# A planned adaLN transformer block on one core: set-up as planned items, new item weights, x+gb*b2 on TensorE, two gelu phases

## The chip, the cores and the metric

One core of a Trainium2 chip runs the whole program. A core has five engines with a queue each: TensorE (PE, matmuls; PEld is its weight load), VectorE (DVE), ScalarE (ACT), GpSimd (POOL) and SyncE (SP, which here only issues DMAs). The metric is the device time of one execution in microseconds, lower is better; for a kernel it is the median of its runs.

## The reference

2048 tokens of width 448, 16 heads of 28, a hidden width of 1792, all bf16. Each token attends to 8 tokens at distances 0, 2, ..., 14 behind it.

```python
mod = (_silu(c) @ w_mod).reshape(c.shape[0], 6, 1, -1)
sa, ca, ga, sb, cb, gb = (mod[:, 0], mod[:, 1], mod[:, 2], mod[:, 3], mod[:, 4], mod[:, 5])
h = _layernorm(x) * (1 + ca) + sa
x = x + ga * _A_ref(h, A_wqkv, A_wo)      # sliding, dilated attention, then @ wo
h = _layernorm(x) * (1 + cb) + sb
x = x + gb * _B_ref(h, B_w1, B_b1, B_w2, B_b2)
# _B_ref: y = layernorm(h); gelu_tanh(y @ w1 + b1) @ w2 + b2
```

## The kernel before

Even tokens come first and odd ones after them, so that the dilated window is a plain window of 8. The 2048 tokens are 16 blocks (b) of 128 on the partitions; attention works on 17 groups (g) of 121 queries with 128 keys; the MLP on 4 chunks (c) of 512 tokens.

Set-up is written out by hand. SP issues the loads of c, x (blocks 0 to 3), wmod (the part for sa and ca), the staging copy of the q and k weights (wqk_st) and Wv. PE turns c into a column (ps_c), DVE and ACT make silu of it, PE multiplies it with wmod (ps_col, line 326), DVE writes ca1_col and sa_col (lines 334 to 337), and DVE and ACT spread wqk_st into Wqk, with 32 columns for each head of 28. Thirteen idle matmuls on zeros (line 270) are placed around this. The other loads (x_all 4 to 15, wmod2, wo, b2, w1, b1, w2) are issued on SP too, and wait for the load of Wv.

Everything after that is a list of items for a planner (class Plan). An item has a name, the engines it could run on with a duration for each, the items it needs, the items it must not start before, and the buffers that it takes or uses. `order` places the items one by one: of those that are ready it takes the one with the earliest start, and among equals the one with the longest tail of durations behind it; where an item may run on two engines it takes the one that ends first. The items are then emitted in the order of their planned starts. On the chip each engine works through its queue in that order, and waits for semaphores. Load times are given to the planner as estimates (LANDS).

The items, by name and line:

- front end of a block pair or four blocks: `fst` statistics of x (385, with the aggregation on 386), `frs` variance plus eps (`tv`, DVE, 392) and its power -0.5 (`rs`, POOL, 395), `z` normalised into zbuf (400), `zt` transposes on PE into `ptr` (430), `h` scale and shift into hT (ACT 438 or DVE 441), `qk` projections into `pq` (452), `qe` copies into qT and kT (376 or 378).
- attention of a group: `lt` logits in 16 small matmuls (522) into two PSUM tiles of tag lt, `ex` two exponentials (ACT 533) into `et`, `mk` product with mask_rest (DVE 542), `pv` values (557) and `ve` their copy into vbuf, `po` the 16 products (567), `on` reciprocal of the denominator and division (DVE 575 and 577), `pt` transposes (584), `ot` copies into oT.
- block: `wo` output projection (605), `x1` residual (DVE 610).
- norms of a pair of blocks: `s2`, `r2`, `z2` (z on 400), `ml` and `ad` (DVE 629: times 1+cb, plus sb), `s3`, `r3`, `y` (ybuf), `yt` a transposing DMA on SP into yT (644).
- MLP of a chunk: `w1` in 7 items of 8 matmuls (660) into PSUM tiles of the tag lt, `ge` gelu (ACT 667) into hm, `w2` in 7 items of 2 matmuls for each block (686), accumulated into p2, `xp` the sum x + gb*b2 (POOL 677) into x1p_ring, `fin` the last sum (DVE 693), `out` the store.
- modulation: `pb_ga`, `pb_sb`, `pb_cb`, `pb_gb` (475); wo is scaled with ga (483, 485), w2 with gb (499).

PSUM has two tiles of tag lt (two banks each), three of tag s and one of tag p2. The last chunk's second to fourth block use tag s for p2. In SBUF `et` has two buffers. The gelus of a chunk are kept in phases: PHASES gives, for each chunk, the number of attention groups whose exponentials come before its gelus.

```python
PHASES = [10, 13, 16, 17]
SLOTS = {"lt": 2, "s": 3, "p2": 1, "et": 2, "on": 2, "vb": 3, "z2": 2, "yT": 2, "hm": 2, "xp": 4}
wait_for(bulk_dmas, wv_loads[1:], "bulk loads after the critical loads")
```

Of the kernel before, what the change touches and what calls it, by code (L numbers as in the profile page):

```python
# [15 lines left out]
KT = 4  # L16
KA = 64
# [14 lines left out]
PHASES = [10, 13, 16, 17]  # L32
# [3 lines left out]
LANDS = [("x0", 5.0), ("mod1", 9.8), ("wq", 10.5), ("wv", 11.0), ("x4", 14.5), ("wmod2", 19.0), ("wo", 20.0),  # L36
         ("b2", 21.0), ("x8", 24.0), ("w1", 29.0), ("w2", 34.0)]
PLANS = None
SCHED = mybir.DependencyInfo(mybir.DependencyClass.NoSync, mybir.DependencyReason.SCHED_ONLY)
# [4 lines left out]
class Plan:  # L44
# [8 lines left out]
    def add(self, name, eng, needs=(), after=(), uses=(), allocs=(), lag=0.09, tab=None, at=0.0, fn=None, pri=0.0):  # L53

        i = len(self.ops)
        self.index[name] = i
        self.ops.append(dict(name=name, eng=eng, needs=list(needs), after=list(after), allocs=list(allocs), lag=lag,
                             tab=tab, at=at, fn=fn, pri=pri))
        for b in list(uses) + list(allocs):
            self.bufs[b][1].append(i)  # L60

    def order(self, hop=0.07, table=1.3):
# [33 lines left out]
        seq = []  # L96
# [10 lines left out]
        while ready:  # L107
# [31 lines left out]
            start[i], end[i], o["ran"] = s, s + o["eng"][e] + o["lag"], e  # L139
            free[e] = s + o["eng"][e]  # L140
# [18 lines left out]
def kernel(  # L159
# [56 lines left out]
    x1p_ring = cst.tile([128, NX1P, D], FP32, name="x1p_ring")  # L216
# [27 lines left out]
    silu_bf = cst.tile([128, KT], BF16, name="silu_bf")  # L244
    wk = ctx.enter_context(tc.tile_pool(name="wk", bufs=2))
# [7 lines left out]
    nc.sync.dma_start(out=x_all[:, 0:2, :], in_=xv[:, 0, 0:2, :])  # L253
    nc.sync.dma_start(out=x_all[:, 2:4, :], in_=xv[:, 0, 2:4, :])
# [4 lines left out]
    load_ktiles(nc.sync, wqk_st, A_wqkv[:, 0:2 * D], 0)  # L259
    wv_loads = load_ktiles(nc.sync, Wv, A_wqkv[:, 2 * D:3 * D], 0)  # L260
# [40 lines left out]
    ps_c = ps_small([128, KT], FP32, "ps_c")  # L301
    for kt in range(KT):
        nk = 128 if kt < KT - 1 else 64
        nc.tensor.matmul(ps_c[0:nk, kt:kt + 1], lhsT=c_row[0:1, kt * 128:kt * 128 + nk], rhs=one1[0:1, 0:1],
                         start=True, stop=True)
    c_col = stp.tile([128, KT], FP32, name="c_col")
    nc.vector.memset(c_col[:], 0.0)
    nc.vector.tensor_copy(out=c_col[:, 0:KT - 1], in_=ps_c[:, 0:KT - 1])
    nc.vector.tensor_copy(out=c_col[0:64, KT - 1:KT], in_=ps_c[0:64, KT - 1:KT])
    e_c = stp.tile([128, KT], FP32, name="e_c")  # L310
    nc.scalar.activation(out=e_c[:], in_=c_col[:], func=ACT.Exp, scale=-1.0)
    nc.vector.tensor_scalar_add(out=e_c[:], in0=e_c[:], scalar1=1.0)
    nc.vector.reciprocal(out=e_c[:], in_=e_c[:])
    nc.vector.tensor_tensor(out=silu_bf[:], in0=e_c[:], in1=c_col[:], op=ALU.mult)

    idle(6)

# [3 lines left out]
    ps_col = ps_small([128, 2 * KT], FP32, "ps_col")  # L321
    for v in range(2):
        for j in range(KT):
            nj = 128 if j < KT - 1 else 64
            for kt in range(KT):
                nc.tensor.matmul(ps_col[0:nj, v * KT + j:v * KT + j + 1],
                                 lhsT=wmod[0:kr_of(kt), kt, v * D + j * 128:v * D + j * 128 + nj],
                                 rhs=silu_bf[0:kr_of(kt), kt:kt + 1], start=(kt == 0), stop=(kt == KT - 1))
    idle(3)
    ca1_col = cst.tile([128, KT], FP32, name="ca1_col")  # L330
    sa_col = cst.tile([128, KT], FP32, name="sa_col")
    nc.vector.memset(ca1_col[64:128, KT - 1:KT], 0.0)
    nc.vector.memset(sa_col[64:128, KT - 1:KT], 0.0)
    nc.vector.tensor_scalar_add(out=ca1_col[:, 0:KT - 1], in0=ps_col[:, KT:2 * KT - 1], scalar1=1.0)
    nc.vector.tensor_scalar_add(out=ca1_col[0:64, KT - 1:KT], in0=ps_col[0:64, 2 * KT - 1:2 * KT], scalar1=1.0)
    nc.vector.tensor_copy(out=sa_col[:, 0:KT - 1], in_=ps_col[:, 0:KT - 1])
    nc.vector.tensor_copy(out=sa_col[0:64, KT - 1:KT], in_=ps_col[0:64, KT - 1:KT])

    for kt in range(KT):
        kr = kr_of(kt)  # L340
        wq_out = Wqk[0:kr, kt, :, :].rearrange("p m (r e) -> p m r e", e=32)[:, :, :, 0:DH]
        wq_in = wqk_st[0:kr, kt, :].rearrange("p (m r d) -> p m r d", m=8, r=4)
        if kt in (0, 2):
            nc.vector.tensor_copy(out=wq_out, in_=wq_in)
        else:
            nc.scalar.copy(out=wq_out, in_=wq_in)
    nc.vector.tensor_copy(out=silu_bc[:], in_=silu_bf[:].unsqueeze(2).to_broadcast([128, KT, 128]))
    bulk_dmas.append(nc.sync.dma_start(out=x_all[:, 4:8, :], in_=xv[:, 0, 4:8, :]))
    bulk_dmas += load_ktiles(nc.sync, wmod2, w_mod[:, 2 * D:6 * D], 0)
    bulk_dmas += load_ktiles(nc.sync, wo_s, A_wo, ZR_N)  # L350
    bulk_dmas.append(nc.sync.dma_start(out=b2_bc[:], in_=B_b2.partition_broadcast(128)))
    bulk_dmas.append(nc.sync.dma_start(out=x_all[:, 8:NBLK, :], in_=xv[:, 1, :, :]))
# [6 lines left out]
    bulk_dmas += load_ktiles(nc.sync, w1_s, B_w1, 0)  # L359
    bulk_dmas.append(nc.sync.dma_start(out=w1_s[KA:KA + 1, KT - 1, :], in_=B_b1.rearrange("(o n) -> o n", o=1)))  # L360
    bulk_dmas.append(nc.sync.dma_start(out=w2_s[:], in_=B_w2.rearrange("(ft p) n -> p ft n", p=128)))
    wait_for(bulk_dmas, wv_loads[1:], "bulk loads after the critical loads")
    stp_cm.__exit__(None, None, None)
    big = ctx.enter_context(tc.tile_pool(name="big", bufs=2))
# [4 lines left out]
    ALL = list(range(KT))  # L369

    def engine(e):
        return nc.vector if e == "DVE" else nc.scalar
# [7 lines left out]
    def stats(nm, tile_key, n, i, src, **kw):  # L380
        def fn(e):
            if i == 0:
                T["mv", tile_key] = sm.tile([128, n, 2], FP32, name="mv", tag=f"mv{n}")
            st = sm.tile([128, 6], FP32, name="st", tag="st")
            nc.vector.bn_stats(out=st[:], in_=src())  # L385
            nc.vector.bn_aggr(out=T["mv", tile_key][:, i, :], in_=st[:])  # L386
        P.add(nm, {"DVE": 0.62}, fn=fn, **kw)
# [21 lines left out]

    zc = [0]  # L410

    def front_end(b0, nb, x_at):
# [4 lines left out]
        rstd(f"frs{b0}", f, nb, needs=[f"fst{b0 + i}" for i in range(nb)])  # L417
# [17 lines left out]
        for kt in range(KT):  # L435
# [8 lines left out]
            P.add(f"h{b0}.{kt}", {"ACT": 0.45 + 0.0004 * w, "DVE": 0.2 + 0.0005 * w},  # L444
                  needs=[f"zt{b0 + i}" for i in range(nb)] + ["mod1"], uses=[f"ptr{b0}"], fn=h_fn)
        h_of[b0] = [f"h{b0}.{kt}" for kt in range(KT)]
        for m in range(8):
# [6 lines left out]
            P.add(f"qk{b0}.{m}", {"PE": 4 * w / 2400}, needs=h_of[b0] + ["wq"], allocs=[f"pq{b0}.{m}"], lag=0.17,  # L454
# [3 lines left out]
            P.add(f"qe{b0}.{m}", {"ACT": 0.06 + w / 1164, "DVE": 0.07 + w / 960}, needs=[f"qk{b0}.{m}"],  # L458
# [6 lines left out]
    front_end(2, 2, "x0")  # L465
# [4 lines left out]
    def mod_item(idx, nm, use, lens):  # L470
# [7 lines left out]
        P.add(nm, {"PE": 0.76}, needs=["wmod2"], allocs=[nm], lag=0.17, fn=fn)  # L478
# [9 lines left out]
    def use_gb(e, pb):  # L488
        nc.vector.tensor_copy(out=gb_bc[:], in_=pb[:])
        nc.vector.tensor_tensor(out=gbb2_bc[:], in0=pb[:], in1=b2_bc[:], op=ALU.mult)  # L490

    mod_item(2, "pb_ga", use_ga, {"DVE": 2.0})
# [3 lines left out]
    mod_item(5, "pb_gb", use_gb, {"DVE": 1.08})  # L496
# [10 lines left out]
    def attention(g, exp_after, lt_after):  # L507
# [5 lines left out]
        for nm, tag in ((f"lt{g}.0", "lt"), (f"lt{g}.1", "lt"), (f"pv{g}", "s"), (f"po{g}", "s"), (f"pt{g}", "s"),  # L513
                        (f"et{g}", "et"), (f"on{g}", "on"), (f"vb{g}", "vb")):
            P.buf(nm, tag)
# [10 lines left out]
        P.add(f"lt{g}", {"PE": 0.45}, after=lt_after, needs=[f"qe{f}.{m}" for f in fes for m in range(8)], lag=0.17,  # L526
# [34 lines left out]
        P.add(f"ve{g}", {"ACT": 0.47, "DVE": 0.54}, needs=[f"pv{g}"], uses=[f"pv{g}", f"vb{g}"],  # L561
# [7 lines left out]
        P.add(f"po{g}", {"PE": 0.45}, needs=[f"mk{g}", f"ve{g}"], uses=[f"et{g}", f"vb{g}"], allocs=[f"po{g}", f"on{g}"],  # L569
              lag=0.17, fn=o_fn)  # L570

        def d_fn(e):
            rden = sm.tile([128, H], FP32, name="rden", tag="rden")
            po = T["po", g]
            nc.vector.reciprocal(out=rden[:], in_=po[:, :, DH])
            on = T["on", g] = wk.tile([128, D], BF16, name="on", tag="on")
            nc.vector.tensor_tensor(out=on[:].rearrange("p (h d) -> p h d", h=H), in0=po[:, :, 0:DH],  # L577
                                    in1=rden[:].unsqueeze(2).to_broadcast([128, H, DH]), op=ALU.mult)
        P.add(f"on{g}", {"DVE": 0.71}, needs=[f"po{g}"], uses=[f"po{g}", f"on{g}"], fn=d_fn)
# [6 lines left out]
        P.add(f"pt{g}", {"PE": 0.24}, needs=[f"on{g}"], uses=[f"on{g}"], allocs=[f"pt{g}"], lag=0.2, fn=p_fn)  # L586
# [132 lines left out]
    for i in todo:  # L719
        o = P.ops[i]  # L720
        if o["fn"]:
            o["fn"](o["ran"])
# [32 lines left out]
```

## Time and profile before

| | |
|---|---|
| median of 3 runs | 216.62 us (216.28 to 218.09) |
| the profiled execution | 217.38 us, span 215.7 us |
| PE busy | 186.4 us (86%) in 1466 matmuls |
| DVE busy | 142.9 us (66%) |
| ACT busy | 111.8 us (52%), 12 table loads among it |
| POOL busy | 45.2 us (21%) |
| p from yT (w1) | 213 records, 52.0 us |
| p from hm (w2) | 224 matmuls, 46.3 us |
| x1p on POOL | 16, 18.9 us |
| statistics (385) and aggregation (386) | 48 each, 29.4 and 8.7 us |
| HBM read and written | 9.18 and 1.84 MB |

The span is the time from the first to the last instruction of the profiled execution; its own time holds a little more around it. A row of the timeline gives the start and the length in us, the engine, the line, the operation, the tiles (written <- read), the number of instructions merged, and in brackets the idle time of the engine before it and what ended that. Matmuls overlap, so that the length of one is more than the step from it to the next; some matmul records are missing (11 of the 224 w1 matmuls).

### The profile page before, as it was taken

The page shows a single profiled execution, that of the slowest core. Times are in us where ns is not written, and L with a number is a line of the kernel's source. Part 1 is how long each engine was busy: PE and PEld are TensorE (multiplying, and loading weights), DVE is VectorE, ACT ScalarE, POOL GpSimd, SP SyncE. Part 2 cuts the span into 40 slices and gives each one's busy share as a digit, 9 for nine tenths or more (in the row PEclk, how much of TensorE's full clock was granted, in tenths as well). Part 3 has the DMA queues.
Part 4 walks back from the last instruction along what each step waited for, and adds up shares of the span by engine and source line. Part 5 has one row for each costly group of instructions (what it writes and reads, how often), then busy time and mean ns, then how long its engine had stood idle before and what let it go on. Part 6 is the DMA issues. An engine that isn't in the chain of part 4 may idle for free.

```text
span 215.7 us, 3681 instructions
## 1 busy us (share of the span) xinstructions
PE 186.4 (86%) x1466; PEld 96.4 (45%) x1481; DVE 142.9 (66%) x327; ACT 111.8 (52%) x142; POOL 45.2 (21%) x72
## 2 busy tenths in 40 slices
PE   7247994999999789988596999998999888999973
PEld 2225862355446335534243454544544443445531
DVE  2076697979999887899998868626788671000232
ACT  3033876373897856859327759467793301531000
POOL 8502010010311020107434401303041151000130
PEclk9755997699999999999979999999999999999999
DMA  4959994000002011000113110110000212000011
GB/s 118 292 152 365 345 292 146 0 0 3 0 2 52 0 27 24 2 3 0 24 25 74 39 34 0 32 38 24 21 24 2 49 48 65 3 0 0 28 61 62
DMA packets 17973, 13.35 MB, mean 62 GB/s; under 512 B 9250, under 2 KB 17059, under 8 KB 17956
## 3 DMA queue, kind: packets, MB, share of 16 engines
q1 hardware_dynamic: 17956, 13.12, 21.2%
q8 instruction: 11, 0.18, 0.3%
q14 instruction: 6, 0.05, 0.1%
HBM read 9.18 MB, written 1.84 MB: 51 GB/s over the span
## 4 chain that ended last, share of the span: by engine, by line
PE 55%; DVE 31%; POOL 4%; DMA 3%; ACT 2%; issue 2%; SPq 1%; POOLq 0%
PE p L686 16%; PE pq L452 13%; PE p L660 12%; DVE st L385 6%; POOL rs L395 4%; PE pv L557 4%; PE pw L605 4%; DVE z L629 3%; DMA wmod<-in_w_mod_dram 3%; DVE x_all L693 3%; DVE z L400 2%; DVE et L542 2%; DVE on L577 2%; DVE mv L386 2%; DVE x_all L610 2%
## 5 line engine op out<-in xcount | busy, mean ns | idle before, releaser
L660 PE MATMUL p<-yT,w_s 128*128 128x512 bf16 x213 | 52.0, 385 | 1.6 <-ACT et L533 0.9
L686 PE MATMUL p<-w_s,hm 128*128 128x448 bf16 x224 | 46.3, 353 | 6.2 <-DVE x_all L693 6.2
L667 ACT ACTIVATE hm<-p 128x1024 bf16<-128x1024 f32 x28 | 28.6, 1023 | 35.9 <-PE p L660 35.7
L395 POOL TENSOR_TENSOR rs<-tv,neg_half 128x2 f32<-128x2 f32 (+1 forms) x21 | 19.3, 923 | 111.3 <-DVE tv L392 111.3
L533 ACT ACTIVATE et<-lt 128x1024 bf16<-128x1024 f32 x34 | 33.4, 1027 | 6.8 <-PE lt L522 6.7
L452 PE MATMUL pq<-hT,Wqk 128*128 128x512 bf16 (+1 forms) x156 | 33.0, 360 | 3.1 <-DVE wo_s L485 1.7
L686 PEld LDWEIGHTS <-hm 128*128 128x128 bf16 x224 | 21.2, 98 | 27.2 <-issue 7.9
L660 PEld LDWEIGHTS <-w_s 128*128 128x128 bf16 x224 | 21.8, 99 | 25.9 <-issue 2.4
L693 DVE TENSOR_TENSOR x_all<-p,x1p_ring 128x448 bf16<-128x448 f32 x16 | 10.0, 623 | 35.0 <-PE p L686 31.4
L677 POOL TENSOR_TENSOR x1p_ring<-x_all,gbb_bc 128x448 f32<-128x448 bf16 x16 | 18.9, 1186 | 52.7 <-DVE x_all L693 49.4
L452 PEld LDWEIGHTS <-Wqk 128*128 128x128 bf16 x160 | 15.9, 104 | 16.9 <-issue 5.0
L542 DVE TENSOR_TENSOR et<-et,mask_rest 128x2048 bf16<-128x2048 bf16 x17 | 21.4, 1258 | 1.0 <-ACT et L533 1.0
L385 DVE BATCH_NORM_STATS2 st<-x_all 128x6 f32<-128x448 bf16 x32 | 19.6, 612 | 0.2
L557 PE MATMUL pv<-Wv,hT 128*128 128x448 bf16 x68 | 15.3, 353 | 0.1
L605 PE MATMUL pw<-wo_s,oT 128*128 128x448 bf16 x64 | 15.2, 362 | 0.2
L610 DVE TENSOR_TENSOR x_all<-pw,x_all 128x448 bf16<-128x448 f32 x16 | 9.9, 617 | 4.5 <-PE pw L605 4.3
L378 ACT CAST kT<-pq 128x512 bf16<-128x512 f32 (+1 forms) x18 | 9.3, 517 | 4.4 <-PE pq L452 4.0
L577 DVE TENSOR_TENSOR on<-po,rden 128x448 bf16<-128x448 f32 x17 | 10.6, 625 | 0.6
L378 ACT CAST vbuf<-pv 128x448 bf16<-128x448 f32 x14 | 7.4, 536 | 6.8 <-PE pv L557 6.7
L438 ACT ACTIVATE hT<-ptr,sa_col,ca_col 128x512 bf16<-128x512 bf16 (+1 forms) x9 | 6.3, 707 | 8.1 <-DVE hT L441 8.1
L522 PE MATMUL lt<-qT,kT 28*128 28x128 bf16 x272 | 7.6, 218 | 2.7 <-DVE hT L441 2.6
L385 DVE BATCH_NORM_STATS2 st<-z 128x6 f32<-128x448 bf16 x16 | 9.8, 611 | 0.1
(89 smaller groups left out, 185.3 us busy)
## 6 DMA issues: line engine op xcount, KB each, us to landing
out_dram<-x_all SPq DMA_DIRECT2D x16, 112.0 KB, 1.7
w_s<-in_B_w_dram SPq DMA_DIRECT2D x1, 1568.0 KB, 13.8
wmod<-in_w_mod_dram SPq DMA_DIRECT2D x1, 1344.0 KB
w_s<-in_B_w_dram SPq DMA_DIRECT2D x1, 1344.0 KB
x_all<-in_A_x_dram SPq DMA_DIRECT2D x1, 896.0 KB, 9.5
wmod<-in_w_mod_dram SPq DMA_DIRECT2D x1, 672.0 KB, 6.8
wqk_st<-in_A_wqkv_dram SPq DMA_DIRECT2D x1, 672.0 KB, 8.5
x_all<-in_A_x_dram SPq DMA_DIRECT2D x2, 224.0 KB, 2.7
```

The costliest lines, as they stand in the source:

```text
L378: nc.scalar.copy(out=out, in_=in_)
L385: nc.vector.bn_stats(out=st[:], in_=src())
L395: nc.gpsimd.tensor_tensor(out=rs[:], in0=T["tv", tile_key][:], in1=neg_half[:, 0:n], op=ALU.pow)
L452: nc.tensor.matmul(pq[:, 0:w], lhsT=Wqk[:, kt, m, :], rhs=hT[:, kt, c0:c0 + w], start=(kt == 0), stop=(kt == KT - 1))
L533: nc.scalar.activation(out=et_v[:, 2 * half:2 * half + 2], in_=T["lt", g][half][:].rearrange("p r (ft c) -> p r ft c", ft=4), func=ACT.Exp ...
L542: nc.vector.tensor_tensor(out=et[:], in0=et[:], in1=mask_rest[:], op=ALU.mult)
L557: nc.tensor.matmul(pv[:], lhsT=hT[:, kt, k0:k0 + BK], rhs=Wv[:, kt, :], start=(kt == 0), stop=(kt == KT - 1))
L605: nc.tensor.matmul(pw[:], lhsT=oT[:, kt, jb * 128:(jb + 1) * 128], rhs=wo_s[:, kt, :], start=(kt == 0), stop=(kt == KT - 1))
L660: nc.tensor.matmul(p1[:, f, 0:w], lhsT=w1_s[:, kt, ft * 128:(ft + 1) * 128], rhs=T["yT", c][:, kt, 0:w], start=(kt == 0), stop=(kt == KT - 1))
L667: nc.scalar.activation(out=T["hm", c][:, 2 * q:2 * q + 2, 0:w], in_=T["p1", c, q][:, :, 0:w], func=ACT.Gelu_apprx_tanh)
L677: nc.gpsimd.tensor_tensor(out=x1p_ring[:, b % NX1P, :], in0=x1_blk(b), in1=gbb2_bc[:], op=ALU.add)
L686: nc.tensor.matmul(T["p2", b][:], lhsT=T["hm", c][:, ft, bi * 128:(bi + 1) * 128], rhs=w2_s[:, ft, :], start=(ft == 0), stop=(ft == FT - 1))
```

## The change

1. Set-up becomes planner items: `ps_c`, `c_col`, `e_c`, `silu`, `idle` (14 idle matmuls, beside the 4 at the beginning), `ps_col`, `mod1`, `silu_bc`, and four items that spread the k weights first (`wk0`, `wk1`) and then the q weights. The x blocks 0 to 3 are loaded by the ACT queue, the k weights before the q weights, and the other loads follow on SP without a wait.
2. A statistic and its aggregation are two items (`fst`/`s2`/`s3` and `ag...`), as are reciprocal and division (`rd`, `on`). A statistic may also run on ACT, as two activations with accumulation and two small products, planned at 2.0 us.
3. x + gb*b2 is no longer made on POOL. gb*b2 is added inside p2 by one more matmul for each block: `share` (all 1/64) times gbb2_rows. The upper 64 rows hold gb*b2 rounded to bf16 and the lower 64 hold what the rounding left. `fin` adds x itself.
4. PHASES puts the exponentials of the groups 10 to 16 behind the gelus of chunk 0, and the gelus of chunks 1 to 3 behind all of them.
5. The planner's tails get a weight by kind of item (PRI), new durations, and a doubled length for PE items that follow a stretch of 3.413 us in which PE has little to do.

In the order that this gives, 47 of the 48 statistics stay on DVE and one goes to ACT; ACT has 4 table loads. The first mask copy on DVE is placed ahead of the copies of ps_c.

```diff
-PHASES = [10, 13, 16, 17]
+PHASES = [10, 17, 17, 17]
+NIDLE = 14
+PRI = {"po": -68.5, "r3": 10.0, "ve": -28.0, "lt": 6.0, "on": -24.0, "w2": -9.0, "ex": -20.0, "zt": 7.0,
+       "r2": 53.3, "ge": -12.0, "w1": -13.0, "yt": 4.0, "y": 6.0, "z2": -7.0, "ml": -1.7, "pb": -5.0, "ot": 3.7,
+       "pt": -0.6, "rd": 1.1, "h": 7.0, "mk": -2.0}
+STATS_ACT = 2.0
...
+            d = o["eng"][e]
+            if e == "PE":
+                w = int(s / win)
+                if pe_busy.get(w - 1, 0.0) < 0.4 * win:
+                    d *= 2
...
-    nc.sync.dma_start(out=x_all[:, 0:2, :], in_=xv[:, 0, 0:2, :])
-    nc.sync.dma_start(out=x_all[:, 2:4, :], in_=xv[:, 0, 2:4, :])
+    nc.scalar.dma_start(out=x_all[:, 0:2, :], in_=xv[:, 0, 0:2, :])
+    nc.scalar.dma_start(out=x_all[:, 2:4, :], in_=xv[:, 0, 2:4, :])
...
-    load_ktiles(nc.sync, wqk_st, A_wqkv[:, 0:2 * D], 0)
-    wv_loads = load_ktiles(nc.sync, Wv, A_wqkv[:, 2 * D:3 * D], 0)
+    load_ktiles(nc.sync, wqk_st[:, :, D:2 * D], A_wqkv[:, D:2 * D], 0)
+    load_ktiles(nc.sync, wqk_st[:, :, 0:D], A_wqkv[:, 0:D], 0)
+    load_ktiles(nc.sync, Wv, A_wqkv[:, 2 * D:3 * D], 0)
+    nc.sync.dma_start(out=x_all[:, 4:8, :], in_=xv[:, 0, 4:8, :])
+    load_ktiles(nc.sync, wmod2, w_mod[:, 2 * D:6 * D], 0)
...
-    wait_for(bulk_dmas, wv_loads[1:], "bulk loads after the critical loads")
...
+        P.add(nm, {"DVE": 0.53, "ACT": STATS_ACT} if STATS_ACT else {"DVE": 0.53}, fn=fn, **kw)
+        P.add("ag" + nm, {"DVE": 0.08}, needs=[nm], fn=a_fn)
...
+    P.add("idle", {"PE": 3.0}, after=["ps_c"], fn=lambda e: idle(NIDLE), pri=50.0)
+    P.add("ps_col", {"PE": 1.3}, needs=["silu", "wmod"], after=["idle"], allocs=["ps_col"], lag=0.2, fn=col_fn)
+    P.add("mod1", {"DVE": 0.3}, needs=["ps_col"], uses=["ps_col"], fn=mod1_fn)
...
+            nc.vector.tensor_tensor(out=gbb2_rows[:], in0=pb[:], in1=b2_bc[:], op=ALU.mult)
+            nc.vector.tensor_tensor(out=gbb2_bc[64:128, :], in0=pb[64:128, :], in1=b2_bc[64:128, :], op=ALU.mult)
+            nc.vector.tensor_tensor(out=gbb2_rows[64:128, :], in0=gbb2_bc[64:128, :], in1=gbb2_rows[64:128, :],
+                                    op=ALU.subtract)
...
-                nc.gpsimd.tensor_tensor(out=x1p_ring[:, b % NX1P, :], in0=x1_blk(b), in1=gbb2_bc[:], op=ALU.add)
...
+                            nc.tensor.matmul(T["p2", b][:], lhsT=share[:], rhs=gbb2_rows[:], start=True, stop=False)
...
-                nc.vector.tensor_tensor(out=x_all[:, b, :], in0=T["p2", b][:], in1=x1p_ring[:, b % NX1P, :],
+                nc.vector.tensor_tensor(out=x_all[:, b, :], in0=T["p2", b][:], in1=x1_blk(b) if XP == "PE" else x1p_ring[:, b % NX1P, :],
                                         op=ALU.add)
```

## Prediction, made before the changed kernel was run

> **What bounds the kernel now.** I read the strip of busy slices first, then the timeline of the start, then the list of waits, then two pieces of timeline where the strip dips. The profiled execution took 217.38 us, its span is 215.7, and the median of the three runs is 216.62: I sum against the span and add 0.92 at the end.
>
> ```profile
> PE   7247994999999789988596999998999888999973
> ...
> DVE  2076697979999887899998868626788671000232
> ...
> PEclk9755997699999999999979999999999999999999
> ```
>
> A slice is 5.4 us. PE is nearly full from slice 5 to the end, so time is won only where PE stands still, works at a lower clock, or has less to do. At the rates the trace shows for unbroken runs (512 columns 0.213, 448 columns 0.187, a group's 16 lt 0.34 and 16 po 0.40), PE's work from the first projection to the last matmul is 163.3 us; it took from 19.3 to 212.3, 193. The 30 us between are the subject, with the 19 before them.
>
> ```profile
> 5.26 0.29 POOL L295 TENSOR_SCALAR_AFFINE_SELECT mask<-mask 128x128 bf16<-128x128 bf16 x1
> ...
> 11.97 0.16 DVE L334 TENSOR_SCALAR ca_col<-ps_col 128x3 f32<-128x3 f32 x1 [7.16 <-PE ps_col L326]
> ...
> 13.79 0.61 DVE L385 BATCH_NORM_STATS2 st<-x_all 128x6 f32<-128x448 bf16 x1
> ...
> 18.63 0.41 DVE L441 TENSOR_SCALAR hT<-ptr,ca_col,sa_col 128x256 bf16<-128x256 bf16 x1
> ```
>
> DVE waits 7.16 us for ps_col with x long landed (2.7 us after its issue at 1.2 and 1.7); only then come Wqk, the mask and the statistics, and the first hT starts at 18.63.
>
> ```profile
> 35.00:40.00 5.00, 3.10 (x20) 1.27 (x22) 4.87 (x8) 2.52 (x3) 0.00 (x0) 0.52 0.00 2
> ...
> 105.00:110.00 5.00, 3.59 (x13) 1.59 (x15) 4.90 (x12) 1.25 (x3) 0.12 (x1) 0.69 0.26 52
> ```
>
> Columns: PE, PEld, DVE, ACT, POOL busy, granted clock, DMA. The clock is 0.52 and 0.69 there, each time after a PE stall.
>
> ```profile
> 99.78 5.04 POOL L677 TENSOR_TENSOR x1p_ring<-x_all,gbb_bc 128x448 f32<-128x448 bf16 x4 [0.43 <-DVE gbb_bc L490]
> 100.75 2.15 DVE L400 TENSOR_SCALAR z<-x_all,mv,rs 128x448 bf16<-128x448 bf16 x2
> ...
> 106.19 0.40 PE L584 MATMUL pt<-ident,on 128*128 128x128 bf16 x4 [1.96 <-DVE on L577]
> ```
>
> While POOL adds x1p, two z take DVE 2.15 (0.70 elsewhere), and PE waits for `on`.
>
> ```profile
> PE p L686 <- DVE x_all L693: 6.2, 7, 1.7
> ```
>
> PE waits 6.2 us in seven places for the one p2 bank to be read out.
>
> **The change, part by part.**
>
> *Start.* DVE's new queue begins, after the memsets, with the mask copy, which waits for POOL (5.26+0.29=5.55). Then by steps of before's rows: mask 0.60, two c_col copies 0.25 (to 6.4), one statistic 0.53 that hides e_c on ACT (to 6.95), three silu steps of 0.21 (7.6), statistic 0.53, silu_bc 0.33, two aggregates 0.2 (8.65), statistic 0.53, tv, aggregate, tv (9.5). POOL's two pow (0.70 and 0.83) run from 9.45 to 11.0; its memsets end at 8.4, plus 0.2 for `share`, which hides them by 0.8. z to 11.35, four half-width Wqk copies of 0.2, ca_col and sa_col 0.3, the fourth z 0.3: first hT at 12.7 instead of 18.63, −5.9. The weights stay early enough: wmod's last part let ps_col go on at 9.54 and 2.4 us later it was done, 11.95, against 12.15 needed; Wqk's staging was complete at 11.8 and its first half is now wanted at 11.35. x's two issues leave SP (wmod 1.0 earlier) for ACT, 0.9 ahead of the table load there; e_c, at 6.4, covers that by 3 us. The bulk issues (8.7 us on SP, 13.09 to 22.3) move to behind Wv; SP's next user is yT at 65.9. The one statistic that goes to ACT (the order has 47 of 48 on DVE) costs about 1.5 us in ACT's wait before 11.8: nothing.
>
> *Clock at the start.* Before, projections ran at half clock from 19.3 until about 21.6 (0.84 granted in 20 to 25: 1.6 us at half), costing 1.1. Now 14 idle matmuls at 0.43, then 0.22, end near 7; then come one-column ps_col and transposes, as before. Nearest row: the same ramp, 0. Ends: −1.1 (clock held) and +2.3 (half clock for the 6.8 us that the dip at 35 lasted).
> The Trainium skill ("TensorE: Matmul & The Clock Gate", the clock-gate part and PE-mode transpose) says that an idle window of some 3.4 us takes the clock back to half and that transposes don't count as busy, which speaks against the 14 idle matmuls; by it the sum would be 0.6 to 2.3 higher. The rows agree in that the clock was 0.50 from 10 to 20 us though three idle matmuls and transposes ran there.
>
> *Stall at 34 to 42.* lt and the 512-wide projections waited for hT and for wo_s's scaling on DVE (1.12 and 1.66), then ran at half clock to 42: 2.8+2.45=5.25 lost. In the new order 24 projections, pb_ga, pv and the transposes lie between the first two lt; DVE still has wo_s (1.46+0.53) ahead of one hT (0.46), 2.45 against some 1.8 of PE work there after pb_ga, and a mask product before it. I leave 1.5; stalls that short (1.49 at 73.17) left the clock at 1.00. −3.75; ends −5.25 and −1.5.
>
> *x1p.* POOL's 16 adds go. The DVE excess there (1.45+0.72+0.83=3.0) cost PE 1.96 and 0.31×5=1.55 of clock: 3.5. The gbb2 item has two more DVE operations (1.06) at the same place, so −3.0; ends −3.5 and −2.0.
>
> *Share matmuls.* 16 of 448 columns at 0.187: +3.0, all on PE, which sets the end.
>
> *p2.* In the new order a group of another bank or w1 lies between blocks, except between the first two. −6.2+1.2=−5.0; ends −5.5 and −4.
>
> *Tables.* Twelve loads become four; 8×1.29=10.3 of ACT. On PE's path only the wait of 0.9 at 97.7 (a late exp holding a lt bank): −0.9; ends −0.9, 0.
> The skill ("ScalarE: Activation LUTs", What ACT_TABLE_LOAD costs) puts a switch at 2.66 us with its drain; the trace shows 1.29 from load to next instruction, so by it ACT would gain 21 instead of 10.3, and nothing on the path changes.
>
> *Statistics apart.* A statistic and its aggregate step by 0.74 now; with something between, 0.63: 47×0.11=5.2 of DVE, and 17 reciprocals free about 0.1 each. Mostly behind PE; of its waits for DVE at 73 and 79 (1.49, 0.95) I take off 1.0; ends −3, 0.
>
> *Two gelu phases.* Between the first w2 of chunk 0 and the first w1 of chunk 1 PE now has 22.8 us of work for seven attention groups: 60 w2 and share matmuls 11.2, pv and pw 6.0, the rest small. DVE's queue from the last w_s product to the last mask product has 28.7 (7 masks 7.9, ten statistics 5.3, six x1 3.2, six `on` 3.2, others 9). It starts earlier, since w2 waits for the first w_s. The 6 that it has more bound the cost: 0 to +6, I take +2.0.
>
> Sum: 215.7−5.9+0−3.75−3.0+3.0−5.0−0.9−1.0+2.0=201.15; plus 0.92, 202.
>
> **The rivals.** *Loads come late.* Bulk loads now share the DMA with wk and wq. x4 and wmod2, 2.0 MB at the 295 GB/s of 5 to 10 us, would hold back hT by up to 6 us if all went in turn: the start's gain is gone, 208. Against: before, all lay in one queue and landed in order of issue (wo_s 22.2, b2 23.5, x8 26.0, w1 31.8, w2 35.7).
> *DVE is the bound from 20 to 120.* Then the PE items at 34 and at 100 and the tables bring nothing: 215.7−5.9−5.0+3.0+2.0=209.8, 211. For: DVE at 9 in most slices there. Against: PE was at 4.9 of 5 us in the same ones.
> *Slower: seven groups alone.* The groups 10 to 16 no longer have w1 work between them, and each passes lt, exp, mask, po, `on`, pt with two lt and two et buffers. Eight lt rows from 46.56 to 92.18 are 6.5 us apart; seven such are 45.6 instead of 24.8: +21, 223. It decides from 6.0 us a group on. Against: those 6.5 contain whole front ends, and the shortest steps were 3.0 and 3.8.
>
> **How the numbers follow.** Forecast 0.66, late loads 0.10, DVE bound 0.13, seven groups 0.11. The forecast's best ends give 194.3, its worst 214.5; the range 194.5 to 212 takes in two rivals and leaves out the third and the worst corner. About 1% (2.2 us) is what a measurement tells from no change: faster 0.86, same 0.05, slower 0.09.
>
> **What would show it.** Right: first hT at 12.5 to 13.5; no 0.5 clock between 25 and 212; waits of p for x_all under 2 us; z pairs at 0.7 throughout; four table loads; first w1 of chunk 1 near 120. Wrong: Wqk or ps_col waiting for DMA past 12.5; lt steps over 5 us among the last seven groups; PE idle before share for gbb_rows.

## The result and the profile after

The changed kernel takes 199.12 us (median of 4 runs, 198.74 to 199.44) beside 217.36 (216.28 to 218.43) for the kernel before: a ratio of 0.916, 95% interval 0.910 to 0.922. Its profiled execution took 199.31, with a span of 197.6 instead of 215.7. The forecast was 202, range 194.5 to 212. One run further below, with four phases and the weights, had two slow executions among its ten, and its median leaves them out.

The strip of busy slices of the changed kernel (a slice is 4.9 us now):

```profile
PE   7949969989899999999989999999999999999993
...
DVE  1877689989798799899879999899711011120021
...
PEclk9975999999999999999999999999999999999998
```

PE's slices of 4 to 7 behind the start are gone but for one 6 (24.7 to 29.6 us, where lt waits for hT). By the rates of unbroken runs PE's work from the first projection to the last matmul is 166.3 us (163.3 before); it takes 180.2 (193 before). One dip is left ahead of the last matmul, the third and fourth digit of PEclk, and it is the one that the sum had not paid for. The timeline of the start (start, length, engine, line, operation, tiles, count, in brackets the idle time before and what ended it):

```profile
5.58 0.95 DVE L560 COPY mask_rest<-mask 128x2048 bf16<-128x2048 bf16 x1 [3.99 <-POOL mask L325]
...
7.35 1.59 POOL L348 MEMSET w_s<- 64x1792 bf16 x1
7.58 0.62 DVE L372 BATCH_NORM_STATS2 st<-x_all 128x6 f32<-128x448 bf16 x1
8.12 1.10 DVE L450 COPY silu_bc<-silu_bf 128x512 bf16<-128x512 bf16 x1
...
12.68 0.15 DVE L435 TENSOR_SCALAR ca_col<-ps_col 128x3 f32<-128x3 f32 x1
13.26 0.40 DVE L493 TENSOR_SCALAR hT<-ptr,ca_col,sa_col 128x256 bf16<-128x256 bf16 x1
```

The statistics no longer stand behind ps_col, and the first hT is at 13.26 instead of 18.63. Then the stretches in which the clock was looked at before, and the two at the first projections (us, busy time of PE, PEld, DVE, ACT and POOL, granted clock, DMA share, GB/s):

```profile
10.00:15.00 5.00, 2.42 (x20) 1.52 (x20) 3.71 (x18) 1.82 (x5) 1.49 (x2) 0.71 1.07 388
15.00:20.00 5.00, 5.00 (x30) 3.73 (x29) 3.84 (x15) 2.46 (x8) 1.01 (x1) 0.60 1.09 328
35.00:40.00 5.00, 5.00 (x52) 3.12 (x51) 4.14 (x13) 3.12 (x6) 1.01 (x1) 1.00 0.00 0
105.00:110.00 5.00, 5.00 (x65) 2.95 (x62) 4.67 (x11) 3.68 (x5) 0.70 (x1) 1.00 0.07 23
```

Both stalls, at 35 and at 105, have their clock back (0.52 and 0.69 before). The list of waits has one entry of PE for the p2 bank in place of seven (6.2 us), and little else in mid-kernel. The longest wait there, 1.13 of the 1.7 us in the first line, is at 27.5:

```profile
PE lt L581 <- DVE hT L493: 1.7, 2, 1.1
...
PE p L750 <- DVE x_all L762: 0.7, 1, 0.7
```

### The profile page after: what moved, and what is told of

Same layout as the page of the kernel before. It is cut to its first block, busy times and chain, and to the rows that moved or that the text cites. A ratio compares the mean times of both kernels' runs of the same rounds, so it can differ in the third digit from the quotient of the medians.

```text
span 197.6 us, 3714 instructions
## 1 busy us (share of the span) xinstructions
PE 184.9 (94%) x1488; PEld 98.1 (50%) x1502; DVE 129.8 (66%) x325; ACT 104.4 (53%) x146; POOL 24.8 (13%) x57
## 4 chain that ended last, share of the span: by engine, by line
PE 71%; DVE 17%; POOL 4%; ACT 3%; issue 3%; DMA 1%; POOLq 0%
PE p L752 20%; PE p L723 17%; PE pq L504 14%; PE pv L616 5%; PE pw L668 4%; DVE st L372 3%; ACT hT L490 3%; PE lt L581 2%; PE po L626 2%; DVE hT L493 2%; PE pt L647 2%; PE p L750 2%; POOL rs L392 2%; DVE x_all L673 2%; PE ptr L482 1%
## 5 line engine op out<-in xcount | busy, mean ns | idle before, releaser
L723 PE MATMUL p<-yT,w_s 128*128 128x512 bf16 x215 | 51.0, 379 | 0.6 <-DMA yT<-ybuf 0.2
L752 PE MATMUL p<-w_s,hm 128*128 128x448 bf16 x224 | 47.1, 352 | 0.0
L762 DVE TENSOR_TENSOR x_all<-p,x_all 128x448 bf16<-128x448 f32 x16 | 9.8, 620 | 46.0 <-PE p L752 46.0
L504 PE MATMUL pq<-hT,Wqk 128*128 128x512 bf16 (+1 forms) x155 | 31.8, 355 | 0.9 <-DVE hT L493 0.5
L392 POOL TENSOR_TENSOR rs<-tv,neg_half 128x2 f32<-128x2 f32 (+1 forms) x21 | 17.1, 818 | 116.5 <-DVE tv L389 115.4
L504 PEld LDWEIGHTS <-Wqk 128*128 128x128 bf16 x160 | 16.0, 105 | 12.3 <-issue 0.8
L601 DVE TENSOR_TENSOR et<-et,mask_rest 128x2048 bf16<-128x2048 bf16 x17 | 20.5, 1207 | 0.1
L372 DVE BATCH_NORM_STATS2 st<-x_all 128x6 f32<-128x448 bf16 x31 | 18.3, 609 | 0.1
L616 PE MATMUL pv<-Wv,hT 128*128 128x448 bf16 x68 | 15.3, 353 | 0.3 <-ACT kT L362 0.3
L362 ACT CAST qT<-pq 128x512 bf16<-128x512 f32 (+1 forms) x19 | 9.5, 509 | 3.1 <-PE pq L504 2.8
L626 PEld LDWEIGHTS <-et 128*128 128x128 bf16 x272 | 9.0, 96 | 3.2 <-DVE vbuf L360 0.8
L626 PE MATMUL po<-vbuf,et 128*128 128x29 bf16 x272 | 9.3, 176 | 0.5 <-DVE vbuf L360 0.5
```

The costliest lines, as they stand in the source:

```text
L362: nc.scalar.copy(out=out, in_=in_)
L392: nc.gpsimd.tensor_tensor(out=rs[:], in0=T["tv", tile_key][:], in1=neg_half[:, 0:n], op=ALU.pow)
L504: nc.tensor.matmul(pq[:, 0:w], lhsT=Wqk[:, kt, m, :], rhs=hT[:, kt, c0:c0 + w], start=(kt == 0), stop=(kt == KT - 1))
L601: nc.vector.tensor_tensor(out=et[:], in0=et[:], in1=mask_rest[:], op=ALU.mult)
L616: nc.tensor.matmul(pv[:], lhsT=hT[:, kt, k0:k0 + BK], rhs=Wv[:, kt, :], start=(kt == 0), stop=(kt == KT - 1))
L626: nc.tensor.matmul(po[:, h, :], lhsT=T["et", g][:, h, :], rhs=vbufs[g % NVB][:, h, :], start=True, stop=True)
```

## The experiments

Two kinds of edit. In the first, the planned order stays and one thing in it is changed (three things in the run at the end); the second plans anew with one rule of the planner changed. Times are medians; the ratio is to the kernel before, timed on the same chip (217.9 to 218.1 in these runs). The changed kernel was timed beside 217.36, so that a difference to its 199.12 comes out up to 0.7 us otherwise by the ratios than by the medians; a difference of less than 1 us needs the trace as well.

**The share matmuls, left out.** gb*b2 is then missing from the result.

```diff
-                        if XP == "PE":
-                            nc.tensor.matmul(T["p2", b][:], lhsT=share[:], rhs=gbb2_rows[:], start=True, stop=False)
...
-                                         rhs=w2_s[:, ft, :], start=(ft == 0 and XP != "PE"), stop=(ft == FT - 1))
+                                         rhs=w2_s[:, ft, :], start=(ft == 0), stop=(ft == FT - 1))
```

> The changed kernel with the same planned order, without the 16 share matmuls: gb*b2 is left out of the result. Theory (PE sets the end from the first projection on): PE has 16 x 0.187 = 3.0 us less, so 199.1 - 3.0 = 196.1. Rival (DVE or a wait sets the end of most stages): 199.1 within 0.5.

196.21 us, ratio 0.901 (0.897 to 0.905): 2.9 less than the changed kernel, for 16 matmuls of 0.187. Time that PE saves in the second half of the kernel comes off the end nearly in full. In the trace the last matmul is 3.3 earlier, but 0.6 of that is there at the first lt, because the half clock at the start lay earlier in this execution (10.93 to 17.76 instead of 12.14 to 18.97).

**x1p on POOL, put back beside it.** POOL adds x + gb*b2 for every block into a ring that nobody reads. One more DVE operation comes with it, a memset of the half of gbb2_bc that the change leaves unwritten; it puts the next item 0.57 later on DVE.

```diff
...
+            nc.vector.memset(gbb2_bc[0:64, :], 0.0)
...
+        done.add(o["name"])
+        if o["name"] in ghost_at:
+            for b in ghost_at[o["name"]]:
+                nc.gpsimd.tensor_tensor(out=x1p_ring[:, b % 4, :], in0=x1_blk(b), in1=gbb2_bc[:], op=ALU.add)
```

> The changed kernel in the same order, with 16 POOL additions of x and gb*b2 into a ring that nobody reads, each placed after the z of its block and after gb*b2 as the old x1p were; nothing waits for them but the last sum's write to x. Theory (POOL additions slow DVE's two-port work: 3.0 us of DVE and 3.5 of PE were lost to them before): z pairs of 1.5 to 2.2 us come back, and the time is 200.5 to 202.5. Rival (the loss before was the order of the work, not the additions): 199.1 within 0.6.

202.82 us, ratio 0.931 (0.927 to 0.936): 3.7 more, just over the upper end expected, though in the trace no one waits for these additions. The timelines of the changed kernel (first row) and of this run (the other two) show how they cost:

```profile
99.39 0.69 DVE L397 TENSOR_SCALAR ybuf<-z,mv,rs 128x448 bf16<-128x448 bf16 x2
...
100.58 2.07 POOL L810 TENSOR_TENSOR x1p_ring<-x_all,gbb_bc 128x448 f32<-128x448 bf16 x2
100.65 2.14 DVE L398 TENSOR_SCALAR ybuf<-z,mv,rs 128x448 bf16<-128x448 bf16 x2 [0.35 <-POOL rs L393]
```

Two normalisations that take 0.69 us in the changed kernel take 2.14 beside POOL's two additions, and end with them. The first four additions (82.46 to 88.21) do the same to a product of w_s (1.92 at 85.39 instead of 1.08) and to an addition of sb (1.29 at 87.41 instead of 0.56). The sums, masks and divisions queued behind on DVE are then late: PE waits 1.59 for the p2 bank at 100.35 and 1.32 for a mask product at 103.98, where the changed kernel waits 0.71 and not at all. The memset of this run has up to 0.6 of the 3.7.

**The first four statistics, back behind ps_col.** tv, rs, z and the transposes go with them.

```diff
     todo = P.order()
+    early = [P.index[n] for n in [f"{k}{b}" for k in ("fst", "agfst", "z", "zt") for b in range(4)] +
+             ["frs0a", "frs0", "frs2a", "frs2"]]
+    at = todo.index(P.index["mod1"])
+    moved = [i for i in todo[:at] if i in early]
+    todo = [i for i in todo[:at + 1] if i not in moved] + moved + todo[at + 1:]
```

> The changed kernel with its order as it is, but the four first statistics, their tv, rs, z and transposes put behind ca_col and sa_col, as they stood before the change. The first hT should move from 13.3 to about 16.3 (three statistics 1.6, aggregates and tv 0.6, rs 0.8, z 0.5 behind mod1 at 11.5 to 12.5, or one activation pair on ACT of 1.5 to 2). Theory (what the start loses goes straight to the end): 202 to 203. Rival (loads or DVE between 20 and 90 absorb it): 199 to 200.

200.47 us, ratio 0.921 (0.916 to 0.926). The start lost 1.9 us, less than expected (first projection at 15.69 instead of 13.79), and the last matmul came 1.7 later, at 195.64 instead of 193.94; the median rose by 1.4 (the four executions lie between 199.85 and 202.05, and the trace is of the one with 202.05). So what the start wins or loses arrives at the end nearly whole, and this move is a part of the 5.4 that the start won. The rest came of the other set-up items and was not taken apart further.

**Idle matmuls up to the first projection.**

```diff
+FILL = {"ps_col": 5, "zt2": 4}
...
         if o["fn"]:
             o["fn"](o["ran"])
+        if o["name"] in FILL:
+            fill_ps = ps_att([128, 512], FP32, "idle_ps")
+            for _ in range(FILL[o["name"]]):
+                nc.tensor.matmul(fill_ps[:], lhsT=idle_in[:, 0:128], rhs=idle_in[:], start=True, stop=True)
```

> Order as in the changed kernel, 9 more idle matmuls: 5 behind ps_col and 4 behind the third block's transposes. Theory: the half clock from 12.9 to 19.7 follows from the PE-poor stretch 9.5 to 12.9; filled, the first projections run at full clock and 1.9 of the 3 us that half clock costs there come off the end: 196.5 to 197.7, with a granted clock over 0.9 from 10 to 20. Rival: the first projections wait for hT and for their copies, and the end stays within 0.4 of 199.1, or the clock drops in spite of them.

197.62 us, ratio 0.908 (0.905 to 0.911): 1.5 less; in the trace the last matmul is 1.9 earlier (192.03). The same two stretches in this run:

```profile
10.00:15.00 5.00, 4.05 (x29) 1.96 (x29) 3.71 (x18) 1.62 (x4) 1.49 (x2) 1.00 1.07 389
15.00:20.00 5.00, 5.00 (x60) 4.15 (x58) 3.84 (x15) 4.21 (x12) 1.01 (x1) 1.00 1.09 330
```

The half clock that this run removes lay at 12.14 to 18.97 in the changed kernel, a little earlier than expected here. The first projection starts no earlier (13.71), but PE does 60 matmuls between 15 and 20 instead of 30. The 14 idle matmuls of the change end at 7.6 us; nine more behind them, none of them in anyone's way, hold the clock. In three of the six executions the granted clock was 1.00, as in this one; in the others it was 0.99, and they took some 0.3 us longer.

**The mask copy, just ahead of the first lt.**

```diff
     todo = P.order()
+    todo.remove(P.index["mask"])
+    todo.insert(todo.index(P.index["lt0"]), P.index["mask"])
```

> Order as in the changed kernel, but the first mask copy (0.95 on DVE, behind the POOL work that ends at 5.55) is moved from the head of DVE's queue to just ahead of the first lt. Theory: c_col, the statistics and z come 0.9 earlier, the first hT at 12.4; since the clock stays at half until 19.7 only half of that is worth anything: 198.2 to 198.8. Rival: ps_col stays behind the 14 idle matmuls, which end at 7.6, and the mask now holds z of block 4 back: 199.1 to 200.

198.22 us, ratio 0.911 (0.907 to 0.915): 0.9 less, at the good end of what was expected, but the reason given falls. The first projection is 1.26 earlier (12.53) and the last matmul 1.1 (192.82), so more than half went through: in its trace the half clock did not stay until 19, it lay earlier too, from 11.0 to 17.8. The trace is of the execution with 199.38, the longest of the six (its span of 197.7 is that of the changed kernel, because the end came 1.2 us later behind the last sum). In four of the other five the granted clock was 0.991, where the changed kernel has 0.980 to 0.983. Over 196 us that is some 3.5 us of half clock instead of 6.7 or more (an estimate from these shares), so part of the 0.9 is the clock and not the mask.

**Statistic and aggregation, reciprocal and division, side by side again.**

```diff
     todo = P.order()
+    for o in P.ops:
+        n = o["name"]
+        if "ag" + n in P.index or n.startswith("rd"):
+            mate = P.index["ag" + n if "ag" + n in P.index else "on" + n[2:]]
+            me = P.index[n]
+            if n.startswith("rd"):
+                todo.remove(me)
+                todo.insert(todo.index(mate), me)
+            else:
+                todo.remove(mate)
+                todo.insert(todo.index(me) + 1, mate)
```

> Order as in the changed kernel, but each aggregation directly behind its statistic and each reciprocal directly ahead of its division, on DVE. Forecast of the prediction: keeping them apart is worth 1.0 us, so 200.1 (ends 199.1 and 202). Rival: DVE has slack wherever PE is full, and it stays within 0.4 of 199.1.

204.68 us, ratio 0.941 (0.938 to 0.943): 5.6 more, beyond the upper end of 202. 1.3 of it is an accident of the start. There the add of e_c now falls on POOL's memset of w1's tail (timeline of this run):

```profile
7.32 1.62 DVE L419 TENSOR_SCALAR e_c<-e_c 128x4 f32<-128x4 f32 x1
7.33 1.59 POOL L348 MEMSET w_s<- 64x1792 bf16 x1
```

An add of 4 columns (0.14 in the changed kernel) takes 1.62, ps_col waits 1.4 for it, and the first projection comes at 15.05, 1.27 later. The other 4.3 grow on the way: lt of the fourth group is 2.6 us later than in the changed kernel, of the fifth 3.1, of the eleventh 4.5, the last matmul 5.9. DVE is busy 136.0 us instead of 129.8; behind the first hT it is 127.4 instead of 122.2, 5.1 more. Most of that are the aggregations (group, busy us, mean ns, idle before; the changed kernel first, then this run):

```profile
L382 DVE BATCH_NORM_AGGREGATE mv<-st 128x2 f32<-128x6 f32 x47 | 6.7, 162 | 0.1
...
L382 DVE BATCH_NORM_AGGREGATE mv<-st 128x2 f32<-128x6 f32 x47 | 8.5, 182 | 1.6
```

A group's busy time counts overlaps with the statistic ahead; without them the aggregations behind the first hT take 3.8 and 8.0 us. With the short idle times ahead of aggregations and divisions, which grow by 2.0, DVE loses some 7 us, about what the prediction had counted (5.2 for 47 pairs and 0.1 for each of 17 reciprocals). The waits show where a part of it goes, the changed kernel first, then this run:

```profile
PE pt L647 <- DVE on L637: 0.4, 1, 0.4
...
PE pt L647 <- DVE on L637: 3.1, 6, 0.9
```

The wait of w1 for yT grows too, from 0.2 to 1.2.

**The other loads, waiting for the load of Wv again.**

```diff
+    wv_loads = load_ktiles(nc.sync, Wv, A_wqkv[:, 2 * D:3 * D], 0)
...
+    wait_for(bulk_dmas, wv_loads[1:], "bulk loads after the critical loads")
```

> Order as in the changed kernel, but the loads of x_all 4 to 15, wmod2, wo, b2, w1, b1 and w2 wait for the load of Wv again. Theory (the prediction put this part at nothing): the first statistic of block 4 is at 15.9 and pb_ga at 23.9, late enough, so it stays within 0.5 of 199.1. Rival: x_all 4 to 7 or wmod2 come late and hold the first 512-wide projections back: 200 to 202.

200.01 us, ratio 0.919 (0.916 to 0.922), whose interval overlaps that of the change. The issues start at 10.72 instead of 7.01, the first projection is at 13.77 (13.79), the last matmul at 193.26 (193.94). No cost can be seen in the trace: from the first lt to the last every group is 0.78 or 0.79 earlier than in the changed kernel, as the half clock lay earlier too (10.56 to 17.39). But the trace is of the execution with 198.64; the other five took 199.38 to 200.58. The 0.9 between the medians (0.7 by the ratios) is more than the 0.5 expected; it is not told from nothing, and the theory is not confirmed.

**Phases and weights, two by two.** Three kernels, planned anew. The first has the weights and the four phases of before; the second two phases and no weights; the third four phases and no weights.

```diff
-PHASES = [10, 17, 17, 17]
+PHASES = [10, 13, 16, 17]
```

> The changed kernel with the four gelu phases of before (10, 13, 16, 17 groups), planned anew: 12 table loads. Theory (two phases cost about 2 us where seven groups run with little w1 work, and save 0.9 by the tables): 197.5 to 199.5. Rival (the two phases are a main part of the gain): 203 or more.

```diff
-                             tab=tab, at=at, fn=fn, pri=pri + PRI.get(re.match(r"[a-z]+([0-9](?=_))?", name)[0], 0.0)))
+                             tab=tab, at=at, fn=fn, pri=pri))
```

> Two gelu phases, planned without the weights by kind. If the weights only tune an order that the two phases already carry, it gives 200 to 206 us, with the first w1 of chunk 1 still near 122 and some p2 waits back. If the gain hangs on the weights, it is 212 or more.

The third has both edits.

> Four gelu phases as before, planned without the weights. Theory: the loss of the run with four phases (217.6) came from weights that were fitted to two phases, so without them four phases cost the planner little: 199 to 207, about as much as two phases without weights. Rival: four phases themselves hold the norms of the last chunk back; then it is 213 or more and over 8 above two phases without weights.

| | four phases | two phases |
|---|---|---|
| no weights | 214.39, ratio 0.985 (0.980 to 0.989) | 223.94, ratio 1.029 (1.024 to 1.034) |
| weights | 217.30, ratio 0.997 (0.993 to 1.001) | 199.12, ratio 0.916 (0.910 to 0.922) |

Each part alone makes it slower, by 9.6 and by 2.9; both together bring 15.3. All four kernels have the rest of the change, the start, the statistics apart and the share matmuls: with four phases and no weights it brings only 3 to 4 us against the kernel before. My theory missed on all three: weights that tune an order which the phases carry, and four phases that lose only because the weights were fitted to two. The rivals held for the first two runs; for the third neither did, since four phases without weights are neither as good as 207 nor behind two phases.

With the weights and four phases the last group is what is late. Its exponentials wait for the gelus of chunk 2, so its lt is at 164.5 instead of 117.8, and the norms of the last chunk follow. Timeline and windows of that run:

```profile
175.51 2.81 PE L752 MATMUL p<-w_s,hm 128*128 128x448 bf16 x14
186.00 0.58 PE L723 MATMUL p<-yT,w_s 128*128 128x512 bf16 x1 [7.68 <-issue]
```

```profile
180.00:185.00 5.00, 0.00 (x0) 0.00 (x0) 1.14 (x6) 0.00 (x0) 0.70 (x1) 0.57 0.24 55
185.00:190.00 5.00, 3.78 (x9) 1.46 (x11) 0.00 (x0) 0.39 (x1) 0.00 (x0) 0.50 0.07 14
```

PE has nothing for 7.7 us, and then the clock is at half. The profile names no semaphore, only "issue", but in the gap lie the last norms: x1 of the last block at 173.5, its two statistics, the last two normalisations into ybuf at 181.35 and their transposing DMAs, issued until 184.7; yT is what w1 needs. What makes up the rest of the 18 us to the changed kernel was not taken apart.

Without weights and with two phases about half of the 24.8 us to the changed kernel are waits for the one p2 bank. The timeline of DVE in that run, and of PE:

```profile
128.50 0.61 DVE L762 TENSOR_TENSOR x_all<-p,x_all 128x448 bf16<-128x448 f32 x1
```

```profile
121.61 1.72 PE L668 MATMUL pw<-wo_s,oT 128*128 128x448 bf16 x8
129.16 0.53 PE L750 MATMUL p<-gbb_rows,share 128*128 128x448 bf16 x1 [5.83 <-DVE x_all L762]
```

w2 of block 0 ends at 102, but the sum that empties its bank runs at 128.5: of what is ready on DVE it has the shortest tail in the plan (only the store is behind it), so the attention and the norms go first. From 102 on PE has only the seven groups, whose masks and norms fill DVE (29.70 of 30 us between 95 and 125, PE 23.61). The first w1 of chunk 1 is at 134.0 instead of 120.1, and w2 of the remaining blocks runs later with nothing between the blocks: ten waits for p2, 12.3 us. In the changed kernel the same sums stand at:

```profile
98.85 0.62 DVE L762 TENSOR_TENSOR x_all<-p,x_all 128x448 bf16<-128x448 f32 x1 [0.61 <-PE p L752]
104.83 0.62 DVE L762 TENSOR_TENSOR x_all<-p,x_all 128x448 bf16<-128x448 f32 x1 [0.19 <-PE p L752]
112.98 0.62 DVE L762 TENSOR_TENSOR x_all<-p,x_all 128x448 bf16<-128x448 f32 x1
```

**Only the last sums and the norms first.** A test of that reading: two phases, no weights, and one rule in their place.

```diff
-                key = (s, -tail[i], i)
+                key = (s, not o["name"].startswith(FIRST), -tail[i], i)
...
+FIRST = ("fin", "s2", "ags2", "r2", "z2", "ml", "ad", "s3", "ags3", "r3", "y", "yt")
```

> Two gelu phases, planned without the weights, but among items with the same earliest start the last sums (fin) and the norms go first. Theory: what the weights buy with two phases is above all that fin empties the one p2 bank and the norms go ahead of the attention queued on DVE; without them PE had only the seven groups from 102 to 129 us. Then it is 206 to 214, against 223.9 without weights, with fin of block 0 before 107 and the first w1 of chunk 1 before 128. Rival: the order of the attention itself is what the weights buy; then it stays over 219.

208.99 us, ratio 0.960 (0.957 to 0.963). The sums of blocks 0 to 3 are now early (timeline of this run):

```profile
102.19 0.62 DVE L763 TENSOR_TENSOR x_all<-p,x_all 128x448 bf16<-128x448 f32 x1
108.35 0.59 DVE L763 TENSOR_TENSOR x_all<-p,x_all 128x448 bf16<-128x448 f32 x1
115.05 0.62 DVE L763 TENSOR_TENSOR x_all<-p,x_all 128x448 bf16<-128x448 f32 x1
```

The first w1 of chunk 1 is at 121.6, and 15.0 of the 24.8 us that the weights bring with two phases are there. Of the other 9.9, eight waits for p2 (6.0 us) are the largest entry: the rule does not put other work between the blocks of the later chunks, as the weights do. How the two halves of the rule share the 15 was not tried.

**A better start.** The fill and the late mask together, with 10 idle matmuls ahead of ps_col, and the memset of w1's tail on DVE.

```diff
-NIDLE = 14
+NIDLE = 10
+FILL = {"ps_col": 4, "zt2": 4}
...
-    nc.gpsimd.memset(w1_s[64:128, KT - 1, :], 0.0)
+    nc.vector.memset(w1_s[64:128, KT - 1, :], 0.0)
...
+    todo.remove(P.index["mask"])
+    todo.insert(todo.index(P.index["lt0"]), P.index["mask"])
```

> Order as in the changed kernel with three edits of the start together: 8 idle matmuls behind ps_col and the third block's transposes (and 10 instead of 14 ahead of ps_col), the mask copy just ahead of the first lt, and the memset of w1's tail (1.59 on POOL, beside which silu_bc took 1.10 and tv 1.24) on DVE, which stands idle from 1.6 to 3.6. If the gains add up (1.5 of the clock, 0.9 of the mask, 0.5 of the memset): 196.0 to 196.6, first hT at 11 to 11.7. If they cover the same wait: 197.0 to 197.7.

196.14 us (6 runs, 195.26 to 197.43), ratio 0.901 (0.898 to 0.905): faster than both kernels, and 3.0 under the changed one, as if the gains add up. From the timeline and the strip of this run:

```profile
1.72 0.81 DVE L349 MEMSET w_s<- 64x896 uint32 x1
...
11.13 0.40 DVE L494 TENSOR_SCALAR hT<-ptr,ca_col,sa_col 128x256 bf16<-128x256 bf16 x1
```

```profile
PEclk9999999999999999999999999999999999999999
```

The memset costs 0.81 where DVE had nothing to do, the first hT is 2.1 us earlier, and no slice is below 9. The trace is of the execution with 195.26. Those with 196.92 and 197.43 had a granted clock of 0.99, some 4 us of half clock by this share, and where they lay is not on record; the one with 196.78 had 1.00, and why it took longer is open.

## Why the prediction was right, step by step

The result lies 2.9 us under the forecast, inside the range, and all the signs that were named for it were seen (first hT at 13.26, z at 0.30 to 0.40 each, four table loads, w1 of chunk 1 at 120.1, no half clock between 25 and the last matmul), none of those against it. By its terms, forecast first (they are not wholly independent, as the table of phases and weights shows):

- *Start, −5.9:* −5.4 (13.26 against 18.63). Two rows were longer than in the sum of steps: silu_bc took 1.10 instead of 0.33, beside POOL's memset, and the mask copy 0.95 instead of 0.60; other steps were shorter. That it reaches the end was shown for the 1.9 us of it that the first statistics have.
- *Clock at the start, 0, ends −1.1 and +2.3:* +0.4 to +0.8. This step was wrong, inside its own ends. I took the ramp of before for the nearest row; but in the change the clock fell again, to half from 12.1 to 19.0, while the projections began at 13.8. Holding it took 1.9 off the last matmul and 1.5 off the median, against the 1.1 that the ramp of before was counted at. By the rule that I had set against the change (the Trainium skill, "TensorE: Matmul & The Clock Gate", "What's actually happening": an idle window of some 3.4 us takes the clock back to half) the estimate was 0.6 to 2.3; the direction held, the size at or a little under its lower end.
- *Stall at 34 to 42, −3.75:* −3.6 (5.25 lost before; 1.33 and 0.35 are left, at 26 to 29, by the rates of unbroken runs). Read from the traces, not tried by itself.
- *x1p, −3.0, ends −3.5 and −2.0:* −3.7 by the run with POOL's additions put back, of which up to 0.6 is that run's memset.
- *Share, +3.0:* +2.9 by the run without them.
- *p2, −5.0:* the waits fell from 6.2 to 0.7, −5.5. As read from the order, w1 or a group lies between the blocks.
- *Tables, −0.9:* four loads of 1.28 us are left, and one PE wait for an exponential of 0.3. Not tried by itself.
- *Statistics apart, −1.0, ends −3 and 0:* this is the term that was mis-sized. −4.3 by the run that joins them, beyond the end. I had the DVE time about right (6.9 counted with the reciprocals, some 7 found) and put most of it behind PE. But a DVE that is at 9 in its strip next to a full PE is no cover: in the joined run six of the 17 `on` were waited for instead of one, 3.1 us instead of 0.4.
- *Two gelu phases, +2.0:* from the first w2 (95.6) to the first w1 of chunk 1 (120.1) 24.5 us pass, 1.7 over PE's 22.8: +1.7.

With these values (+0.8 for the clock, and −0.9 kept for the tables) the terms add up to −18.0, where the span fell by 18.1. That they meet so well is in part luck: they depend on each other, some are read from the end of the kernel and some from a stretch of it, and the clock and x1p are known to within about 0.5 only. The forecast was too high mainly because of the statistics (3.3). A small slip in the range: its best ends add up to 194.5, not 194.3.

The rivals. *Loads come late* did not happen: the only such wait, of ACT for its half of Wqk, ended at 9.47, four us ahead of the first projection, and holding the loads back costs nothing that shows in the trace. *DVE is the bound from 20 to 120* was half true: the gains at 34 and 100 came, but the run with joined statistics says that some 7 us lost on DVE cost 4.3. *Seven groups alone* did not happen: lt of the last seven are 2.7 to 4.2 us apart. Yet 223 us, its number, is nearly what two phases give without the weights (223.94), and not by its mechanism: there the groups are 2.2 to 4.3 apart, and what stands still is the p2 bank. I had read "a group of another bank or w1 lies between blocks" off the order and priced the phases at +2.0 beside it; that this order needs the weights, and that either part by itself loses, I had not seen. The price was right for the order and would have been wrong for each part.

## What to carry to other kernels

A planner's weights and its constraints have no price one by one: read the order that they give together, and look first for who empties the only buffer of its kind, because a longest-tail rule can put that step last, as it did here. Where two engines are full in the same slices, 0.1 us saved at each of some sixty dependent pairs on the second one is worth more than half of its sum (4.3 of some 7 here). In these runs the idle matmuls held the clock only when they reached up to the first real work; nine in the gaps just before it did what 14 at the beginning did not.

## What the runs showed of the hardware

Read in steps of 0.6 us, the half clock lies at 12.14 to 18.97 in the changed kernel, 11.00 to 17.83 with the late mask and 13.63 to 20.46 with the late statistics: 6.83 us each time, with edges that move. Other stretches are shorter or longer: 3.41 (13.77 to 17.18 without weights), 10.24 (180.71 to 190.95 with four phases and weights) and 13.65 (7.92 to 21.57 in the kernel before), and all 19 stretches of half clock that end ahead of the last matmul in the 14 traces are one, two, three or four times 3.41. The Trainium skill ("TensorE: Matmul & The Clock Gate", "What's actually happening") describes a free-running window of about 3.4 us; the rows agree, and by this the length of a dip is a whole number of windows. Where the windows lie differs from execution to execution: with the same order and the first projection at 13.8, the dip began at 12.14 in the changed kernel, at 10.93 without the share matmuls and at 10.56 with the loads held back, and the first lt then came 0.6 and 0.8 earlier.

The window ahead of a fall was not idle here. Without the share matmuls, the clock fell at 10.93, and in the 3.42 us before PE was busy for 3.25 in 38 matmuls: the last idle ones and all 32 one-column matmuls of ps_col. In this run a string of one-column matmuls did not hold the clock.

Some DVE operations can stand still for the whole of a POOL instruction, however small they are: e_c's 128x4 add took 1.62 us beside a memset of 1.59, two z 2.14 beside two additions of 2.07, and silu_bc 1.10 beside the same memset, while the statistic at 7.58 in the middle of it took its usual 0.62. The Trainium skill ("SBUF — State Buffer", "Who interferes with whom") puts this down to an exclusive lock on a port pair that copies and tensor_scalar can take in their two-port modes, and says that the second to issue waits for the end of the first. The rows agree in length, and in that the statistic is spared; who was first they do not settle for e_c, which by its row started 0.01 ahead of the memset that it waited for. Beside copies and tensor_scalars of DVE, a memset on POOL is therefore to be placed like an operation of DVE.
